# Cached attention on one core: loads in cycles of 16 units, the remainder's P transposed by DMA, and scores up to 14 units ahead

## The chip, the cores and the metric

The kernel runs on one core of one Trainium2 chip. The metric is the device time of one execution in microseconds (us). A core has five engines with a queue of instructions each: PE (matrix multiplication and transposes, with its weight loads shown apart as PEld), DVE (vector operations), ACT (exponential, scaled copies), POOL (elementwise work) and SP, which here only issues loads. They meet through semaphores. Transfers are carried out by 16 DMA engines that are shared by all queues.

## The reference

Two problems of the same shape, A and B, are computed, and their results are put side by side:

```python
B, Sq, D = 16, 144, 448
H, Sk, Dh = 16, 512, 256
q = (x @ wq).reshape(B, Sq, H, Dh).transpose(0, 2, 1, 3)
scores = jnp.einsum("bhqd,bhkd->bhqk", q, k_cache) * (Dh ** -0.5)
p = softmax(scores, axis=-1)
o = jnp.einsum("bhqk,bhkd->bhqd", p, v_cache)
o.transpose(0, 2, 1, 3).reshape(B, Sq, H * Dh) @ wo      # [16, 144, 448]
...
return jnp.concatenate([a, b], axis=-1)                  # [16, 144, 896]
```

All inputs are bf16. Each problem has 64 MB of K and 64 MB of V.

## The kernel before

A **unit** is one head of one batch: 144 queries against 512 keys of 256 elements. There are NT = 512 units, 256 of A and then 256 of B. Four units share one load of V (a group G, 128 of them), eight share one load of K (a supergroup SG, 64 of them).

The 144 queries are more than the 128 rows of PE, so each unit is split: its first 112 queries (QA) have scores of their own, and the remaining 32 (QB) of four units are packed into one set of 128 rows. For one unit PE does, by the names that the program gives its pieces:

- **Q**: the query projection, 8 matmuls (L411), evacuated and scaled by DVE (L425) or ACT (L429).
- **SA**: scores of the 112 queries, 2 matmuls 128x512 (L536) into one of two PSUM banks `sa_ps`. Then the negated maximum on DVE (L548), the exponential with its sum on ACT (L559), the reciprocal on DVE (L569), and the normalization on POOL (L577).
- **TA**: 4 transposes of the normalized P (L590), into the `sa_ps` bank of the unit's parity, and a copy to `pt_sb` by DVE (L600).
- **PV**: P times V, 8 matmuls (L623), evacuated by ACT into `ring` (L638).
- **OP**: the output projection, in pieces of 2 matmuls 128x448 (L661), spread by a credit (`OP_RATE`, 2.25 matmuls a slot), evacuated (L679), and stored.

The packed remainder has, for each supergroup, **SB** (16 matmuls, L459) and, for each group, maximum (L473), exponential (L483), reciprocal (L493), normalization on POOL (L501) and **TB**: 4 transposes of `pb_sb` on PE (L513), then a copy by DVE into `pt_sb` (L522). So there are 128 TBs, 512 transposes.

The order on every engine is written out by one loop over slots (`while True` near the end of the function). In slot i, PE does Q of unit i + LQ = i + 15, SA of unit i + LS = i + 5, TA of unit i + LT = i + 2, and PV of unit i. `_Sched.add` records the reads and writes of each piece, and derives the semaphore waits.

Loads have all one queue, SP, in the order of `dma_plan`. Each has a deadline in slots, an earliest slot `lo` (when its buffer comes free) and a lead; the plan sorts them by deadline. K comes by `dma_start_transpose` (L379) into one of three buffers, V by plain loads (L392) into one of three, x transposed for four batches at a time (L299, L300) into one of three. The weights wq (L277, L279) and wo (L287) of B replace those of A as their parts come free. Stores of finished rows (L691) go out from POOL's queue, and the last two from SP's.

At the start K of 16 units and the first x are loaded as they lie and transposed on PE (KT, L359; XT, L336, in three parts, the last in slot 10), and PE begins with matmuls on zeros (W0, L440) that read `ident` from POOL and `pt_sb`, which DVE clears (L254, `warmz`); DVE also clears a quarter of `wq_sb` (L259, `wqz`).

Of the kernel before, what the change touches and what calls it, by code (L numbers as in the profile page):

```python
# [122 lines left out]
def bass_concat_heads__mha_block_cached__gqa_block_cached__near_ridge_kernel(  # L123
# [18 lines left out]
    NP = 2  # L142
# [7 lines left out]
    NG = NT // 4  # L150
    HG = H // 4
# [9 lines left out]
    LQ, LS, LT = 15, 5, 2  # L161
    LSB = 7
    NKT = 16
    N_WARM = (10, 6)
    NK, NV, NXG = 3, 3, 3
    XB = 4 if Bn % 4 == 0 else (2 if Bn % 2 == 0 else 1)
    NQT, NPA, NPB, NPT, NST, NSTB, NOST = 12, 5, 2, 8, 4, 2, 3
# [5 lines left out]
    NSG = NT // 8  # L173
# [4 lines left out]
    with contextlib.ExitStack() as es:  # L178
# [9 lines left out]
        kt_sb = sb("kt_sb", [128, NK, KR, 2, 8 * SK // KR], BF16)  # L188
        v_sb = sb("v_sb", [128, NV, 4, 4 * DH], BF16)
# [3 lines left out]
        pb_sb = sb("pb_sb", [128, NPB, SK], BF16)  # L193
        pt_sb = sb("pt_sb", [128, NPT, 4, SQ], BF16)
        ost_sb = sb("ost_sb", [128, NOST, D], BF16)
        ident = sb("ident", [128, 128], BF16)
        ones = sb("ones", [128, 128], BF16)
# [8 lines left out]

        S = _Sched()
        kt0_nat = kt_sb[:, 2].rearrange("p k d r -> p (k d r)").rearrange("p (u c e) -> p u c e", u=8, c=4)
        wo_flat = wo_sb[:].rearrange("p c e -> p (c e)")
        kt1_nat = wo_flat[:, 0:8 * 4 * DH].rearrange("p (u c e) -> p u c e", u=8, c=4)  # L210
        x_nat = wo_flat[:, 8 * 4 * DH:8 * 4 * DH + 5 * D].rearrange("p (t e) -> p t e", t=5)
        kt_nat = (kt0_nat, kt1_nat)
        sem_names = list(COMPUTE) + ["ostt0", "ostt1", "xn0", "xn1", "kn0", "kn1", "kn2", "kn3"]
        for i in range(NK):
            sem_names.append("kt%d" % i)
# [8 lines left out]
        for i in range(NOST):  # L224
            sem_names.append("ost%d" % i)
        sems = {n: es.enter_context(nc.semaphore("s_" + n)) for n in sem_names}
# [10 lines left out]

        NEG, RSUM, RINV = 0, NST, 2 * NST
# [3 lines left out]
        def t_ident():  # L242
            def e1(g):
                return g.memset(ones[:], 1.0)
            S.add(POOL, e1, writes=[("ones", 0)], name="ones")

            def e2(g):
                return g.affine_select(ident[:], ones[:], pattern=[[1, 128]], compare_op=ALU.is_equal,
                                       fill=0.0, base=0, channel_multiplier=-1)
            S.add(POOL, e2, reads=[("ones", 0)], writes=[("ident", 0)], name="ident")  # L250

# [30 lines left out]
        def t_load_wo(pr, wg):  # L282
            c0 = wg * WOG
            w = wos[pr]

            def e(q):
                return q.dma_start(wo_sb[:, c0:c0 + WOG, :],  # L287
                                   w[c0 * 128:(c0 + WOG) * 128, :].rearrange("(c p) n -> p c n", p=128)).then_inc(
                    sems["wo%d" % wg], 16)
            x = [(("kn", 2), 1), (("kn", 3), 1), (("xn", 0), 1), (("xn", 1), 1)] if pr == 0 else []  # L290
            S.add(SP, e, writes=[(("wo", wg), pr)] + x, dma_sem="wo%d" % wg, name="wo%d.%d" % (pr, wg))

        def t_load_x(XG):
# [7 lines left out]
            S.add(SP, e, writes=[(("xt", sl), XG)] + ([(("xt2", 0), 1)] if XG == NXG else []), dma_sem="xt%d" % sl, n_dma=2, name="x%d" % XG)  # L301

        def t_load_x_nat(k):
            x = xs[0][0:XB].rearrange("b q d -> (b q) d")
            sem = sems["xn%d" % k]

            def e(q):
                if k == 0:
                    return q.dma_start(x_nat[:, 0:3, :], x[0:384, :].rearrange("(t p) d -> p t d", p=128)).then_inc(
                        sem, 16)  # L310
                q.dma_start(x_nat[:, 3, :], x[384:512, :]).then_inc(sem, 16)
                return q.dma_start(x_nat[0:XB * SQ - 512, 4, :], x[512:XB * SQ, :]).then_inc(sem, 16)
            S.add(SP, e, writes=[(("xn", k), 0)], dma_sem="xn%d" % k, n_dma=1 + k, name="xn%d" % k)
# [10 lines left out]
        def t_xt(k):  # L324
            key, bank, acc = ((("sbb", 0), "sb0", ptb_ps[0]), (("sbb", 1), "sb1", ptb_ps[1]),
                              ("opp", "op", op_ps.bitcast(BF16)))[k]
            c0, n = ((0, 256), (256, 128), (384, XB * SQ - 384))[k]
            dst = acc[:, 0:4 * n].rearrange("p (c r) -> p c r", c=4)

            def e(t):  # L330
                ins = None
                for r0 in range(0, n, 128):
                    m = min(128, n - r0)
                    for kc in range(4):
                        d0 = min(128 * kc, D - 128)
                        ins = t.transpose(dst[:, kc, r0:r0 + m], x_nat[0:m, (c0 + r0) // 128, d0:d0 + 128],  # L336
                                          ident[0:m, 0:m])
                return ins
            S.add(PE, e, reads=[(("xn", k // 2), 0), ("ident", 0)], writes=[(key, ("x", k))], banks=[bank], name="XT%d" % k)

            def ev(v):
                o = xt_sb[:, 0, :, c0:c0 + n]
                return v.activation(o, dst, AF.Copy) if k == 1 else v.tensor_copy(o, dst)
            S.add(ACT if k == 1 else DVE, ev, reads=[(key, ("x", k))], writes=[(("xt2" if k == 2 else "xt", 0), 0)], banks=[bank],
                  name="ext%d" % k)

        def t_kt(u):
# [18 lines left out]
            def ev(v):  # L366
                o = kt_sb[:, u // 8].rearrange("p k d r -> p (k d) r")[:, :, (u % 8) * 128:(u % 8 + 1) * 128]
# [4 lines left out]
        def t_load_k(SG):  # L372
            pr, b, h = unit(8 * SG)
            r0 = b * H + h
            sl = SG % NK
            src = ks[pr].rearrange("b h k d -> (b h k) d")[r0 * SK:(r0 + 8) * SK, :]

            def e(q):
                return q.dma_start_transpose(kt_sb[:, sl].rearrange("p k d r -> p (k d) r"),  # L379
                                             src.rearrange("(r k) d -> r (k d)", k=KR)).then_inc(sems["kt%d" % sl], 16)  # L380
# [5 lines left out]
        def t_load_v(G):  # L386
            pr, b, h0 = unit(4 * G)
            sl = G % NV
            src = vs[pr][b, h0:h0 + 4].rearrange("u (p c) d -> p u (c d)", p=128)

            def e(q):
                return q.dma_start(v_sb[:, sl, :, :], src).then_inc(sems["v%d" % sl], 16)  # L392
            S.add(SP, e, writes=[(("v", sl), G)], dma_sem="v%d" % sl, name="v%d" % G)

# [3 lines left out]
        def t_q(U):  # L398
# [7 lines left out]
            def e(t):  # L406
                ins = None
                for kc in range(4):
# [6 lines left out]
            S.add(PE, e, reads=[(("wq", hg), pr), ("wqz", 0), (("xt", xsl), XG)]  # L415
                  + ([(("xt2", 0), 0)] if XG == 0 and b > 1 else []),
                  writes=[(key, ("q", U))], banks=[bank], name="Q%d" % U)

        def t_evac_q(U):
# [3 lines left out]
            if (U - LQ) % 8 in (2, 4, 6, 7):  # L423
# [7 lines left out]

        def kt_of(U, dc):
            n = SK // KR
            return kt_sb[:, (U // 8) % NK, :, dc, (U % 8) * n:(U % 8 + 1) * n]
# [9 lines left out]

        def kt_keys(us):
            if us[0] < NKT:
                return [(("ktn", u), 0) for u in us]
            return [(("kt", us[0] // 8 % NK), us[0] // 8)]

        def t_sb(SG):  # L450
            ksl = SG % NK

            def e(t):
                ins = None
                for dc in range(2):
                    for jj in range(8):
                        U = 8 * SG + jj
                        j = jj % 4
                        ins = t.matmul(sb_ps[jj // 4][32 * j:32 * j + 32, :].rearrange("q (k r) -> q k r", k=KR),  # L459
                                       lhsT=qt_sb[:, U % NQT, dc, QA:SQ],  # L460
                                       rhs=kt_of(U, dc), start=(dc == 0), stop=(dc == 1),
                                       tile_position=(0, 32 * j))
# [15 lines left out]
        def t_exp_b(G):  # L478
            sl = G % NSTB
            psl = G % NPB  # L480

            def e(a):
                return a.activation(pb_sb[:, psl, :], sb_ps[G % 2][:, :], AF.Exp,  # L483
# [3 lines left out]
                  writes=[(("pb", psl), (G, 0)), (("rsumb", sl), G)], banks=["sb%d" % (G % 2)], name="exb%d" % G)  # L487
# [8 lines left out]
        def t_norm_b(G):  # L496
            sl = G % NSTB
            psl = G % NPB

            def e(g):  # L500
                return g.tensor_tensor(pb_sb[:, psl, :], pb_sb[:, psl, :],  # L501
                                       stat[:, RINVB + sl:RINVB + sl + 1].to_broadcast([128, SK]), op=ALU.mult)
            S.add(POOL, e, reads=[(("pb", psl), (G, 0)), (("rinvb", sl), G)], writes=[(("pb", psl), (G, 1))],
                  name="nmb%d" % G)

        def t_tb(G):
            psl = G % NPB

            def e(t):
                src = pb_sb[:, psl, :].rearrange("q (c p) -> q c p", c=4)  # L510
                ins = None
                for c in range(4):
                    ins = t.transpose(ptb_ps[G % 2][:, c * 128:(c + 1) * 128], src[:, c, :], ident[:, :])  # L513
                return ins
            S.add(PE, e, reads=[(("pb", psl), (G, 1)), ("ident", 0)], writes=[(("sbb", G % 2), ("t", G))],
                  banks=["sb%d" % (G % 2)], name="TB%d" % G)

        def t_evac_ptb(G):
            s0 = (4 * G) % NPT

            def e(v):
                return v.tensor_copy(pt_sb[:, s0:s0 + 4, :, QA:SQ],  # L522
                                     ptb_ps[G % 2][:, 0:512].rearrange("p (c j q) -> p j c q", c=4, j=4))
            S.add(DVE, e, reads=[(("sbb", G % 2), ("t", G))],
                  writes=[(("ptb", (4 * G + j) % NPT), 4 * G + j) for j in range(4)], banks=["sb%d" % (G % 2)],
                  name="eptb%d" % G)

        def t_sa(U):
            SG = U // 8
            ksl = SG % NK  # L530
# [51 lines left out]
        def t_ta(U):  # L582
            psl = U % NPA
            bank = U % 2
# [10 lines left out]
        def t_evac_pta(U):  # L595
            sl = U % NPT
            bank = U % 2
# [15 lines left out]
        def t_pv(U):  # L613
            G, j = divmod(U, 4)
            vsl = G % NV
# [3 lines left out]
            def e(t):  # L619
                ins = None  # L620
                for dc in range(2):
                    for c in range(4):
                        ins = t.matmul(ot_ps[ob][:, dc * SQ:(dc + 1) * SQ],  # L623
                                       lhsT=v_sb[:, vsl, j, c * DH + dc * 128:c * DH + (dc + 1) * 128],
# [60 lines left out]
        def t_store(r):  # L685
            pr, row0, m = chunk_rows(r)
            sl = r % NOST
            sem = "ostt%d" % tail_chunks.index(r) if r in tail_chunks else "ost%d" % sl

            def e(q):  # L690
                return q.dma_start(of[row0:row0 + m, pr * D:(pr + 1) * D], ost_sb[0:m, sl, :]).then_inc(  # L691
                    sems[sem], 16)
            S.add(SP if r in tail_chunks else POOL, e, reads=[(("ost", sl), r)], dma_sem=sem, name="st%d" % r)
# [3 lines left out]
        t_warm_zero()  # L697
        t_wqzero()
        t_ident()
# [252 lines left out]
```

## Time and profile before

| what | us |
|---|---|
| median of 3 runs (1189.49 to 1192.02) | 1189.74 |
| the profiled execution | 1193.1 |
| its span, first to last instruction | 1191.4 |
| ACT busy | 754.9 |
| POOL busy | 676.3 |
| PE, 512 transposes of TB (L513) by their mean of 218 ns | 111.6 |
| POOL, 128 normalizations of the remainder (L501) | 132.9 |
| K, issue to landing, min / median / max | 10.6 / 15.0 / 21.1 |
| V, issue to landing, min / median / max | 5.1 / 6.0 / 15.4 |

The granted clock of TensorE was 1.000 over the whole span. A matmul's duration as listed (218 ns for a TB transpose) covers its way through the array, and matmuls follow each other faster than that: what one costs on PE is read from start to start on the timeline. Waits of SP are mostly those for a buffer to come free. In rows of the timeline a bracket holds the idle time of the engine before the instruction and what ended it; "x4" means four instructions shown as one row.

### The profile page before, as it was taken

To read this page: it belongs to the slowest core of one execution; us is meant where nothing else is said; L and a number is where in the kernel's file an instruction comes from. 1 tells how busy PE (TensorE), PEld (TensorE's weight loads), DVE (VectorE), ACT (ScalarE), POOL (GpSimd) and SP (SyncE) were. 2 spreads that over 40 slices of the span, in tenths; PEclk is the share of its full clock that TensorE was granted. 3 is DMA by queue.
4 is the path that set the end of the run, shared out by engine and by line. 5 is a ranking of instruction groups with operands and counts; after the bars stand their busy time and mean duration, and the time that the engine had idled before them with its cause. 6 is when DMAs were issued, how large, how long until landed. Compare 5 with 4: busy or idle time off the path is not lost.

```text
span 1191.4 us, 34160 instructions
## 1 busy us (share of the span) xinstructions
PE 1178.3 (99%) x14116; PEld 902.6 (76%) x14116; DVE 776.0 (65%) x2192; ACT 754.9 (63%) x2220; POOL 676.3 (57%) x680
## 2 busy tenths in 40 slices
PE   8999999999999999999989999999999999999998
PEld 6777777777777777777767777777777777777775
DVE  5766667666666666666666666666766666666564
ACT  4766666666666666666656666666666666666564
POOL 2555556565565565565555655655655656656553
PEclk9999999999999999999999999999999999999999
DMA  9999999999989999999999999999999999998971
GB/s 343 235 298 279 272 270 234 243 243 253 255 219 246 229 264 249 221 235 244 273 281 286 270 279 277 249 238 233 248 254 234 231 243 250 248 236 238 238 190 48
DMA packets 611146, 294.09 MB, mean 247 GB/s; under 512 B 529712, under 2 KB 538736, under 8 KB 610992
## 3 DMA queue, kind: packets, MB, share of 16 engines
q1 hardware_dynamic: 609360, 288.01, 103.1%
q0 software_dynamic: 1632, 3.90, 1.0%
q8 instruction: 112, 1.84, 0.6%
q14 instruction: 42, 0.34, 0.1%
HBM read 153.61 MB, written 4.13 MB: 132 GB/s over the span
## 4 chain that ended last, share of the span: by engine, by line
PE 95%; DMA 2%; DVE 2%; ACT 0%; issue 0%; SPq 0%; POOL 0%; DVEq 0%; POOLq 0%
PE ot_ps L623 20%; PE qp_ps L411 20%; PE sa_ps L536 19%; PE op_ps L661 17%; PE sa_ps L590 8%; PE sb_ps L459 5%; PE sb_ps L513 2%; DMA kt_sb<-in_A_k_cache_dram 2%; DVE stat L548 1%; DMA wq_sb<-in_B_wq_dram 1%; PE sa_ps L440 0%; PE qp_ps L661 0%; PE op_ps L411 0%; DVE pt_sb L600 0%; DVE stat L473 0%; PE ot_ps L359 0%
## 5 line engine op out<-in xcount | busy, mean ns | idle before, releaser
L577 POOL TENSOR_TENSOR pa_sb<-pa_sb,stat 112x512 bf16<-112x512 bf16 x512 | 531.8, 1039 | 504.1 <-DVE stat L569 503.9
L559 ACT ACTIVATE pa_sb<-sa_ps,stat 112x512 bf16<-112x512 f32 x512 | 351.9, 687 | 404.7 <-DVE stat L548 403.4
L548 DVE TENSOR_REDUCE stat<-sa_ps 112x1 f32<-112x512 f32 x512 | 354.0, 691 | 328.4 <-PE sa_ps L536 327.7
L411 PEld LDWEIGHTS qp_ps<-xt_sb,wq_sb 128*128 128x128 bf16 x4000 | 281.9, 98 | 79.1 <-issue 3.5
L623 PE MATMUL ot_ps<-pt_sb,v_sb 128*128 128x144 bf16 x4096 | 340.5, 226 | 0.0
L411 PE MATMUL qp_ps<-xt_sb,wq_sb 128*128 128x144 bf16 x4000 | 331.8, 226 | 3.1 <-DMA wq_sb<-in_B_wq_dram 3.1
L536 PE MATMUL sa_ps<-kt_sb,qt_sb 128*112 128x512 bf16 x1024 | 310.1, 384 | 1.7 <-ACT pa_sb L559 0.7
L661 PE MATMUL op_ps<-wo_sb,ring 128*128 128x448 bf16 x1120 | 280.6, 352 | 0.0
L623 PEld LDWEIGHTS ot_ps<-pt_sb,v_sb 128*128 128x128 bf16 x4096 | 268.5, 97 | 0.4
L590 PEld LDWEIGHTS sa_ps<-ident,pa_sb 112*128 112x128 bf16 x2048 | 146.7, 97 | 108.2 <-ACT pa_sb L559 21.1
L638 ACT ACTIVATE ring<-ot_ps 128x288 bf16<-128x288 f32 (+8 forms) x512 | 189.9, 371 | 4.5 <-PE ot_ps L623 4.5
L600 DVE COPY pt_sb<-sa_ps 128x448 bf16<-128x448 bf16 x512 | 190.8, 373 | 2.4 <-PE sa_ps L590 2.4
L590 PE MATMUL sa_ps<-ident,pa_sb 112*128 112x112 bf16 x2048 | 185.4, 212 | 0.1
L425 DVE TENSOR_SCALAR qt_sb<-qp_ps 128x288 bf16<-128x288 f32 x247 | 112.8, 457 | 65.9 <-PE qp_ps L411 65.1
L501 POOL TENSOR_TENSOR pb_sb<-pb_sb,stat 128x512 bf16<-128x512 bf16 x128 | 132.9, 1038 | 0.7 <-DVE stat L493 0.7
L536 PEld LDWEIGHTS sa_ps<-kt_sb,qt_sb 128*112 128x112 bf16 x1024 | 97.2, 129 | 37.8 <-issue 27.2
L429 ACT ACTIVATE qt_sb<-qp_ps 128x288 bf16<-128x288 f32 x253 | 104.5, 413 | 15.9 <-PE qp_ps L411 14.8
L661 PEld LDWEIGHTS op_ps<-wo_sb,ring 128*128 128x128 bf16 x1120 | 94.7, 98 | 25.6 <-ACT ring L638 0.2
L559 ACT ACTIVATION_READ_ACCUMULATOR pa_sb<-sa_ps,stat 112x1 f32 x512 | 99.0, 193 | 0.0
L483 ACT ACTIVATE pb_sb<-sb_ps,stat 128x512 bf16<-128x512 f32 x128 | 88.4, 690 | 0.0
L473 DVE TENSOR_REDUCE stat<-sb_ps 128x1 f32<-128x512 f32 x128 | 87.2, 681 | 0.0
L569 DVE RECIPROCAL stat<-stat 112x1 f32<-112x1 f32 x512 | 78.4, 153 | 0.5 <-ACT pa_sb L559 0.5
(49 smaller groups left out, 426.3 us busy)
## 6 DMA issues: line engine op xcount, KB each, us to landing
v_sb<-in_A_v_cache_dram SPq DMA_DIRECT2D x64, 1024.0 KB, 6.0
v_sb<-in_B_v_cache_dram SPq DMA_DIRECT2D x64, 1024.0 KB, 6.0
out_dram<-ost_sb POOLq DMA_DIRECT2D x34, 112.0 KB, 6.1
wo_sb<-in_A_wo_dram SPq DMA_DIRECT2D x8, 448.0 KB, 8.1
wo_sb<-in_B_wo_dram SPq DMA_DIRECT2D x8, 448.0 KB, 6.9
wq_sb<-in_A_wq_dram SPq DMA_DIRECT2D x4, 768.0 KB, 11.0
wq_sb<-in_B_wq_dram SPq DMA_DIRECT2D x4, 768.0 KB, 7.6
kt_sb<-in_A_k_cache_dram SPq DMA_DIRECT2D x2, 1024.0 KB, 8.8
```

What stands on the lines that cost most here:

```text
L411: ins = t.matmul(acc[:, dc * SQ:(dc + 1) * SQ], lhsT=wq_sb[:, kc, c0:c0 + 128], rhs=xt_sb[:, xsl, kc, xo:xo + SQ], start=(kc == 0 and dc = ...
L425: return v.tensor_scalar(qt_sb[:, sl, :, :], src, 1.0 / 16.0, None, op0=ALU.mult)
L501: return g.tensor_tensor(pb_sb[:, psl, :], pb_sb[:, psl, :], stat[:, RINVB + sl:RINVB + sl + 1].to_broadcast([128, SK]), op=ALU.mult)
L536: ins = t.matmul(sa_ps[bank][0:QA, :].rearrange("q (k r) -> q k r", k=KR), lhsT=qt_sb[:, U % NQT, dc, 0:QA], rhs=kt_of(U, dc), start=(dc = ...
L548: return v.tensor_reduce(stat[0:QA, NEG + sl:NEG + sl + 1], sa_ps[bank][0:QA, :], axis=AX.X, op=ALU.max, negate=True)
L559: return a.activation(pa_sb[0:QA, psl, :], sa_ps[bank][0:QA, :], AF.Exp, bias=stat[0:QA, NEG + sl:NEG + sl + 1], scale=1.0, accum_out=stat ...
L577: return g.tensor_tensor(pa_sb[0:QA, psl, :], pa_sb[0:QA, psl, :], stat[0:QA, RINV + sl:RINV + sl + 1].to_broadcast([QA, SK]), op=ALU.mult)
L590: ins = t.transpose(pta_ps[bank][:, c * 128:c * 128 + QA], src[:, c, :], ident[0:QA, 0:QA])
L600: return v.tensor_copy(pt_sb[:, sl, :, 0:QA], pta_ps[bank][:, 0:512].rearrange("p (c q) -> p c q", c=4)[:, :, 0:QA])
L623: ins = t.matmul(ot_ps[ob][:, dc * SQ:(dc + 1) * SQ], lhsT=v_sb[:, vsl, j, c * DH + dc * 128:c * DH + (dc + 1) * 128], rhs=pt_sb[:, sl, c, ...
L638: ins = a.activation(ring[:, 2 * h:2 * h + 2, c0:c0 + n1], src[:, :, 0:n1], AF.Copy)
L661: ins = t.matmul(acc[0:m, 0:D], lhsT=ring[:, c, col0:col0 + m], rhs=wo_sb[:, c, :], start=(c == first), stop=(c == last))
```

## The change

- **P of the remainder by DMA.** TB stays on PE only in supergroups 0 to 9 and 28 to 37 (`TB_SG`). In the other 44, `t_ptb_dma` transposes both groups' `pb_sb` (128 rows of 1024) from SBUF to SBUF into one buffer `pbt_sb`, issued on SP. From supergroup 6 on (`NDIR`), `t_copy_ptb` on POOL copies each group from `pbt_sb` to `pt_sb`; where TB stays after that, DVE's copy goes to `pbt_sb` too.
- **Lead of the scores.** SA runs ahead of PV by `LAGS`: 5 up to supergroup 5, then one more for each supergroup up to 14. For this the 8 SAs of each of nine supergroups lie in 7 slots, so that one slot of each holds two. `NPA` grows from 5 to 14. Q of unit u is in the slot of SA of unit u - 8, or in slot u - 15 if that is earlier. TA's bank is that opposite to the last SA (`ta_bank`).
- **Loads.** From supergroup 10 on (slot 76) a written-out cycle of 16 units: P(n), K(n+2), P(n+1), K(n+3), four V, and x every 32 units. K has three buffers up to supergroup 8 and then two, V three and then five, in one tensor `kv_sb`. x comes two batches at a time in two buffers. Stores are issued on SP, in three slots of each 16.
- **Weights of B.** wo is loaded at slots 277 and 293, and B's output projection starts no earlier than slot 290. `OP_RATE` becomes 2.5.
- **Start.** The third part of XT is gone (the first x has 288 rows), `ones` lies in `pa_sb`, and `t_warm_zero` is called behind `t_wqzero` and `t_ident`.

Counted in the orders of the two programs, PE has 88 TBs and one XT fewer, DVE 2103 pieces in place of 2192, POOL 758 in place of 676, and SP 314 in place of 229.

```diff
-    LQ, LS, LT = 15, 5, 2
-    LSB = 7
+    LT = 2
+    LS = 5
+    LAGS = (5, 5, 5, 5, 5, 5, 6, 7, 8, 9, 10, 11, 12, 13, 14)
+    RAMP = 10
+    NDIR = 6
+    TB_SG = set(range(RAMP)) | set(range(NSG // 2 - 4, NSG // 2 + 6))
+    NK, NV, NXG = 2, 5, 2
+    K3 = 8
+    WO_AT = (277, 277, 293, 293)
+    OP_FROM = (0, 34)
-    NK, NV, NXG = 3, 3, 3
-    XB = 4 if Bn % 4 == 0 else (2 if Bn % 2 == 0 else 1)
-    NQT, NPA, NPB, NPT, NST, NSTB, NOST = 12, 5, 2, 8, 4, 2, 3
+    XB = 2
+    NQT, NPA, NPB, NPT, NST, NSTB, NOST = 12, 14, 2, 8, 4, 2, 3
+    NPBT = 1
...
+        def k_slot(SG):
+            return SG % 3 if SG <= K3 else (SG - K3 - 1) % 2
+
+        def v_slot(G):
+            return G % 3 if G < 2 * K3 + 2 else (G - 2 * K3 + 1) % 5
...
+        def t_ptb_dma(SG):
+            psl = SG % NPB
+            tsl = SG % NPBT
+
+            def e(q):
+                return q.dma_start_transpose(pbt_sb[:, tsl, :, :, :].rearrange("p g c q -> p (g c) q"),
+                                             pb_sb[:, psl, :, :].rearrange("p g k -> p (g k)")).then_inc(
+                    sems["pb%d" % tsl], 16)
...
-        def t_evac_ptb(G):
+        def t_evac_tb(G):
+            tsl = (G // 2) % NPBT
             s0 = (4 * G) % NPT
...
+            if G < 2 * NDIR:
...
+            else:
+                def e(v):
+                    return v.tensor_copy(pbt_sb[:, tsl, G % 2, :, :],
+                                         ptb_ps[G % 2][:, 0:512].rearrange("p (c q) -> p c q", c=4))
...
+        def t_copy_ptb(G):
+            tsl = (G // 2) % NPBT
+            s0 = (4 * G) % NPT
+
+            def e(g):
+                return g.tensor_copy(pt_sb[:, s0:s0 + 4, :, QA:SQ],
+                                     pbt_sb[:, tsl, G % 2, :, :].rearrange("p c (j q) -> p j c q", j=4))
...
-            bank = U % 2
+            bank = ta_bank[U]
...
-            S.add(SP if r in tail_chunks else POOL, e, reads=[(("ost", sl), r)], dma_sem=sem, name="st%d" % r)
+            S.add(SP, e, reads=[(("ost", sl), r)], dma_sem="ost%d" % sl, name="st%d" % r)
...
-        t_warm_zero()
         t_wqzero()
         t_ident()
+        t_warm_zero()
+        ta_bank = {}
+        lag = [LAGS[min(n, len(LAGS) - 1)] for n in range(NSG)]
+        grp_slot = [8 * n - lag[n] for n in range(NSG)] + [8 * NSG - lag[-1] + 4]
+        sb_slot = list(grp_slot)
+        sb_slot[1] = 4
+        sa_slot = [grp_slot[u // 8] + (u % 8) * (grp_slot[u // 8 + 1] - grp_slot[u // 8]) // 8 for u in range(NT)]
...
+        q_slot = [min(sa_slot[max(u - 8, 0)], u - 15) for u in range(NT)]
...
+        for wg in range(NWG):
+            plan(WO_AT[wg // 2], s_min, NU + OP_FROM[1] + wg, t_load_wo, 1, wg)
+        for n in range(RAMP, NSG, 2):
+            t = 8 * n
+            XG = (t + 32) // (XB * H)
+            if (t + 32) % (XB * H) == 0 and XG < NXGT:
+                plan_x(t - (20 if XG == Bn // XB + 2 else 4), XG)
+            plan_pb(t - 4, n)
+            if n + 2 < NSG:
+                plan_k(t - 3, n + 2)
+            plan_pb(t + 2, n + 1)
+            if n + 2 < NSG:
+                plan_k(t + 2, n + 3)
+            for j, at in enumerate((5, 5, 5, 8)):
+                if 2 * n + 3 + j < NG:
+                    plan_v(t + at, 2 * n + 3 + j)
+        for hg in range(HG):
+            lo = q_slot[NU - H + 4 * hg + 3] + 1
+            plan((4.9, 4.9, 8, 16)[hg] + NU - 32, lo, q_slot[NU + 4 * hg], t_load_wq, 1, hg)
...
-        OP_RATE = float(NCH * NWO) / NU
+        OP_RATE = 10.0 / 9 * NCH * NWO / NU
...
-            while stores and stores[0][1] <= i:
+            while stores and stores[0][1] <= i and (i % 16 in (9, 10, 11) or i >= NT - 4):
                 t_store(stores.pop(0)[0])
...
+            if i % 8 == 7 and NDIR * 8 <= i + 1 < NT:
+                t_copy_ptb((i + 1) // 4)
+            if i % 8 == 1 and NDIR * 8 <= i < NT:
+                t_copy_ptb((i + 3) // 4)
...
             if 0 <= u < NT:
+                ta_bank[u] = 1 - last_sa % 2 if sas else u % 2
                 t_ta(u)
...
-                            queue_chunk(r, i + OP_DELAY)
+                            queue_chunk(r, max(i + OP_DELAY, pr * NU + OP_FROM[pr]))
...
-            if i == 10:
-                t_xt(2)
```

## The prediction

> **What bounds the kernel now.** I read the busy line first, then the chain of waits, then what PE waited for.
>
> ```profile
> span 1191.4 us, 34160 instructions
> PE 1178.3 (99%) x14116; PEld 902.6 (76%) x14116; DVE 776.0 (65%) x2192; ACT 754.9 (63%) x2220; POOL 676.3 (57%) x680
> ...
> PE 95%; DMA 2%; DVE 2%; ACT 0%; issue 0%; SPq 0%; POOL 0%; DVEq 0%; POOLq 0%
> ```
>
> PE is busy 99% of the span and carries 95% of the chain: an instruction taken from PE is a gain, a wait given to PE is a loss, and nothing else counts. The waits of PE, the longest first:
>
> ```profile
> PE qp_ps L411 <- DMA wq_sb<-in_B_wq_dram: 3.1, 1, 3.1
> PE sb_ps L459 <- DMA kt_sb<-in_A_k_cache_dram: 1.7, 1, 1.7
> PE sa_ps L440 <- POOL ident L248: 1.5, 1, 1.5
> ```
>
> So only two loads are late in the whole run. The second limit is close, though. The DMA view cut to 254 to 290 us, 0.9 us a slice:
>
> ```profile
> DMA  5499979949699999899999999099999999908999
> GB/s 8 104 290 290 204 230 341 400 178 48 173 407 405 307 290 214 117 221 286 289 288 290 290 291 154 7 330 366 385 380 400 373 361 291 274 6 197 290 290 291
> ```
>
> K's transposes run at 290 GB/s, V's loads at 360 to 400, and between the kinds stand slices of 48, 7 and 6 GB/s. The packets show these as stalls of all 16 engines of about 1.45 us, when a plain load gives way to a transpose or an instruction fetch falls into one: 89 over the run, 118 us, thus 3.7 us per 16 units.
>
> **What is removed.** A unit's slot on the timeline, with a TB and without:
>
> ```profile
> 713.28 0.36 PE L590 MATMUL sa_ps<-ident,pa_sb 112*128 112x112 bf16 x4
> 713.47 0.39 PE L513 MATMUL sb_ps<-ident,pb_sb 128*128 128x128 bf16 x4
> 713.70 0.66 PE L623 MATMUL ot_ps<-pt_sb,v_sb 128*128 128x144 bf16 x8
> ...
> 715.51 0.36 PE L590 MATMUL sa_ps<-ident,pa_sb 112*128 112x112 bf16 x4
> 715.71 0.67 PE L623 MATMUL ot_ps<-pt_sb,v_sb 128*128 128x144 bf16 x8
> ```
>
> The TB holds PE from 713.47 to 713.70, 0.23 us. 44 of 64 supergroups lose two each: 88 x 0.23 = -20.2. XT2's 8 transposes go, at TA's 0.05 each: -0.4. The waits of 3.1 (wq of B) and 1.7 (K of unit 40) are counted out, and what comes in their place is counted below: -4.8. DVE's 88 evacuations (0.41 each) go at no gain by themselves, DVE being 65% busy. Together -25.4.
>
> **What is added on PE's path.**
>
> *Start.* W0 needs `warmz`, which moves behind `wqz` on DVE:
>
> ```profile
> 0.97 0.30 DVE L254 MEMSET pt_sb<- 128x288 uint32 x1
> ...
> 1.52 4.42 PE L440 MATMUL sa_ps<-pt_sb,ident 128*128 128x512 bf16 x10 [1.52 <-POOL ident L248]
> 1.64 1.76 DVE L259 MEMSET wq_sb<- 64x2048 uint32 x1 [0.37 <-issue]
> ```
>
> Now 0.97 + 1.76 + up to 0.37 + 0.30 gives 3.0 to 3.4 in place of 1.52. PE waits for no load at the start (no such row above), so all of it counts: +1.7 (0 to 1.9).
>
> *Ramp of the lead.* From 5 to 14, one per group: 9 slots hold two SAs, and the TA of that slot goes into the bank of the first. How long a bank is taken:
>
> ```profile
> 700.92 0.59 PE L536 MATMUL sa_ps<-kt_sb,qt_sb 128*112 128x512 bf16 x2
> 701.55 0.69 DVE L548 TENSOR_REDUCE stat<-sa_ps 112x1 f32<-112x512 f32 x1 [0.47 <-PE sa_ps L536]
> 702.28 0.69 ACT L559 ACTIVATE pa_sb<-sa_ps,stat 112x512 bf16<-112x512 f32 x1 [0.48 <-DVE stat L548]
> 702.87 0.19 ACT L559 ACTIVATION_READ_ACCUMULATOR pa_sb<-sa_ps,stat 112x1 f32 x1
> ```
>
> Free at 703.06, 2.14 after SA's start. PE meanwhile has SA, Q, SA = 0.43 + 0.50 + 0.43 = 1.36 (starts on the timeline), so it waits 0.8; in the first two groups no Q stands between, 0.86, so 1.3. 7 x 0.8 + 2 x 1.3 = +8.2 (0 if the bank were another one; at most 9 x 1.3 = 11.7).
>
> *Slots without an OP piece.* In PE's two orders, between units 8 and 488, 73 slots have none before, 109 after (OP_RATE 2.5 in place of 2.25, B's pieces held back to unit 290). Such a slot has Q 0.50, SA 0.43, TA 0.20, PV 0.50 = 1.63 us on PE. DVE needs 0.63 to the max, 0.69 for it, 0.37 for the TA's copy, 0.15 for a reciprocal: 1.84. So 0.2 x 36 = 7.2. From the other side: the gaps over 0.1 us before SA sum to 6.6 us over the 73 slots, 0.09 each, so 3.3. I take +7, nearer the chain, because DVE's queue has no slack where such slots follow each other; ends 0 and 14.
>
> *Tail.* The last 14 slots, not 5, have no Q and SA: TA 0.20 and PV 0.50 against copies of 0.37 and 0.40 with hand-overs of some 0.2. Nine more slots at 0 to 0.45: I take +2.
>
> **DMA.** New are 44 transposes of P (256 KB) on SP, 116 POOL copies, and 2 K buffers for 3. No row shows an SBUF-to-SBUF transpose. Lower end: 1024 packets at K's rate (8192 in 7.3 us) 0.9 us. Upper end: a stall of 1.45 on either side, 3.8. In the packets of 268.27 us, K follows x's transpose without a gap, so I take 0.9. A cycle of 16 units then needs 2 x 7.3 (K) + 2 x 0.9 (P) + 4 x 2.7 (V) + 3.7 (stalls) + 0.9 (x, store) = 31.8 us, against 16 x 2.268 (mean slot, units 112 to 216) - 4 x 0.23 = 35.4. It fits, with 3.6 us to spare, but with two buffers K(n+2) must land within 9 slots of its release, about 20 us, and it waits on SP behind P(n), which itself waits for the POOL copy; behind them queue P(n+1), K(n+3) and four V. K's present landing:
>
> ```profile
> L379 SPq DMA_TRANSPOSE kt_sb<-in_B_k_cache_dram x32: 7880/12758/17200, 573.8 to 1136.4; - x32
> ...
> DMA to landing us min/median/max: 10.6/15.0/21.1
> ```
>
> Ordinary cycles hold: 15.0 + 0.9 of 20. Three places don't. At unit 40, K5 was 1.7 late and now has one piece of x and its stall more in its way: 3. At SG 32, wq of B (three loads of 0.9 MB before K32, 2.4 each at V's rate) makes 39 us of a 36 us cycle: 3.5. At SG 38, four loads of wo (1.2 each) make 36.6 of 35.4, after a queue already late: 2.5. Sum +9; ends 0 (queue ahead everywhere) and 25 (each 8 late, K's landing spread and a stall). PV of 80 waits for the first copy, as the first P follows four V: +1.5 (0 to 3).
>
> The POOL copies (about 1 us by its norm's 1038 ns) cost nothing: POOL is 57% busy and 14 units of lead cover it; without that cover each late copy would hold the norms behind it, then TA.
>
> The Trainium skill, page "DMA: Bandwidth & Descriptors", section "Anatomy of one DMA — SWDGE (gpsimd) path", puts about 2.0 us of fixed cost on each DMA beside its bytes, and the section "Latency and other measured facts" gives a DMA transpose 261 GB/s. By both, an estimate for P is 3.0 us, and the sum would end with the third case below. The trace disagrees on the rate (290 here), and the gapless packets at 268.27 us speak against a fixed part that holds the engines.
>
> **Sum.** -25.4 + 1.7 + 8.2 + 7 + 2 + 9 + 1.5 = +4.0: span 1195.4. The profiled execution was 1.7 over its span and the median 1.7 below the span, so the median comes to 1193.7; I say 1194.
>
> **Rivals.**
> 1. *No load is late.* Grouping by kind halves the changes from plain to transpose; K32 lands in time if two of its stalls fall away. Then the 9 falls and the OP-free slots cost their measured 3.3: 1194 - 9 - 3.7 = 1181 to 1185, say 1184 (1176 to 1187). For: slack of 3.6 us a cycle. Against: K5 was already late. It decides once K of SG 32 and 38 land before their SB.
> 2. *DMA becomes the bound.* From P = 0.9 + 3.6/2 = 2.7 us a cycle is longer than its 16 slots, and every cycle ends in a wait of SB for K. At 3.0 us, 0.6 x 22 cycles = 13: 1207; at 3.5 us, 1.6 x 22: 1229. I say 1209 (1203 to 1229). For: 103% of the DMA time is already taken on the main queue. Against: the gapless packets. This is also the case of the skill's fixed cost.
> 3. *It does not do what it says*: P lands so late that the copies, the norms and TA follow each other; the gain of 20.2 is paid back in TA's waits: about 1192.
>
> **How the numbers follow.** Forecast 0.48, own range 1188 to 1201 (slower 0.35, same 0.11, faster 0.02). No load late 0.28 (faster 0.26, same 0.02). DMA bound 0.19, all slower. The last 0.05 (same 0.02, slower 0.03). Under 0.2%, 2.4 us, a measurement of this kernel tells no difference. The range reaches from inside the first rival, 1181, to 1213.
>
> **What would show it.** PE's instructions 352 fewer and its busy time about 20.6 lower; first matmul at 3.2; nine TA waits on ACT of about 0.8 between units 40 and 110; SB waits for K at units 40, 256 and 304 and nowhere else; P's packets spanning about 0.9 us. Wrong if SB waits for K every 16 units (rival 2), or never (rival 1), or if TA waits on POOL (rival 3).

## The result: 1.2% slower, and the profile after

| | before | after |
|---|---|---|
| median, us | 1189.74 (1188.88 to 1192.02, 5 runs) | 1204.10 (1200.88 to 1205.55, 5 runs) |
| profiled execution / its span, us | 1193.1 / 1191.4 | 1204.98 / 1203.3 |
| PE busy, us | 1178.3 | 1170.9 |
| K, issue to landing, min / median / max, us | 10.6 / 15.0 / 21.1 | 9.7 / 12.1 / 21.3 |

The ratio after to before is 1.0115, with an interval of 1.0096 to 1.0134. The same lines of the page as before, then what PE waited for (us in total, times, longest):

```profile
span 1203.3 us, 33501 instructions
PE 1170.9 (97%) x13756; PEld 881.1 (73%) x13756; DVE 751.3 (62%) x2103; ACT 753.8 (63%) x2220; POOL 721.2 (60%) x762
...
PE 83%; DMA 8%; DVE 4%; POOL 3%; ACT 1%; issue 1%; SPq 0%; DVEq 0%
```

```profile
PE sa_ps L628 <- ACT pa_sb L597: 7.8, 10, 1.2
PE sb_ps L474 <- DMA kv_sb<-in_B_k_cache_dram: 6.9, 3, 3.5
PE sb_ps L474 <- DMA kv_sb<-in_A_k_cache_dram: 4.1, 3, 2.4
PE sa_ps L453 <- DVE pt_sb L276: 3.5, 1, 3.5
```

PE has 360 instructions fewer (352 of TB, 8 of XT), yet its part of the chain fell from 95% to 83%: DMA, POOL, DVE and ACT now end what PE waits for. The first two kinds of wait are new or have grown. PE's busy time fell by only 7.4 us, although 19.8 us of TBs are gone: some 12 us of the gaps found below lie under the listed durations of matmuls and count as busy.

To find all of it, I took from both traces, for each piece of PE, the time from its start to the next piece's start, less the pace that the same pair keeps when nothing holds it (SA 0.43, Q 0.50, TA 0.20, PV 0.50, an OP piece 0.38, SB 0.98). These excesses sum to 23.1 us before and 54.3 after:

| excess of PE, us | before | after |
|---|---|---|
| between the two SAs of a double slot and TA | 0 | 8.5 |
| ahead of SB (K) | 1.9 | 11.9 |
| ahead of Q of unit 268 (wq of B) | 3.3 | 0 |
| ahead of PV of unit 80 (first POOL copy) | 0 | 0.8 |
| slow clock behind two K waits | 0 | 3.3 |
| small waits of 0.05 to 0.3 elsewhere, most ahead of SA or Q where no OP piece stands | 3.7 | 10.7 |
| after unit 480 | 2.2 | 4.6 |
| below 0.05 each, the first 24 units and others | 12.0 | 14.5 |

So 31.2 us of new gaps stand against 19.8 us of removed TBs (88 x 0.225) and nearly equal small changes at the start. The spans differ by 11.9.

The largest new wait, in the timeline of a double slot, where the two SAs are those of units 56 and 57:

```profile
144.67 0.64 PE L574 MATMUL sa_ps<-kv_sb,qt_sb 128*112 128x512 bf16 x2
145.14 0.66 PE L429 MATMUL qp_ps<-xt_sb,wq_sb 128*128 128x144 bf16 x8
145.64 0.59 PE L574 MATMUL sa_ps<-kv_sb,qt_sb 128*112 128x512 bf16 x2
146.90 0.37 PE L628 MATMUL sa_ps<-ident,pa_sb 112*128 112x112 bf16 x4 [0.67 <-ACT pa_sb L597]
```

TA could start at 145.64 + 0.43 = 146.07 and starts at 146.90. The trace puts the end of its wait down to ACT's exponential of the first SA, whose sum is read out until 146.85.

And what nobody had counted, in windows of 2 us around SB of units 256 and 304 (columns: length, busy time and instructions of PE, PEld, DVE, ACT, POOL; then the granted clock, DMA share and GB/s):

```profile
592.00:594.00 2.00, 0.21 (x4) 0.15 (x8) 0.00 (x0) 0.00 (x0) 0.00 (x0) 1.00 1.10 273
594.00:596.00 2.00, 2.00 (x18) 0.72 (x11) 0.00 (x0) 0.00 (x0) 0.00 (x0) 0.52 1.01 315
596.00:598.00 2.00, 2.00 (x17) 1.54 (x16) 1.47 (x4) 0.74 (x3) 0.63 (x1) 0.63 0.99 125
598.00:600.00 2.00, 2.00 (x26) 1.61 (x25) 1.17 (x3) 1.01 (x4) 0.41 (x1) 1.00 1.38 106
...
706.00:708.00 2.00, 1.77 (x17) 0.67 (x18) 0.00 (x0) 0.00 (x0) 0.00 (x0) 0.68 1.27 290
708.00:710.00 2.00, 2.00 (x15) 1.62 (x14) 1.23 (x4) 0.50 (x1) 0.39 (x1) 0.50 1.27 290
```

PE stands for want of K and, when it goes on, runs at about half the clock for some 3 us: 15 to 18 matmuls in 2 us in place of 26.

### The profile page after: what moved, and what is told of

Its sections match the earlier page's. It is cut to its first block, busy times and chain, and to the rows that moved or that the text cites. A ratio compares the mean times of both kernels' runs of the same rounds, so it can differ in the third digit from the quotient of the medians.

```text
span 1203.3 us, 33501 instructions
## 1 busy us (share of the span) xinstructions
PE 1170.9 (97%) x13756; PEld 881.1 (73%) x13756; DVE 751.3 (62%) x2103; ACT 753.8 (63%) x2220; POOL 721.2 (60%) x762
## 4 chain that ended last, share of the span: by engine, by line
PE 83%; DMA 8%; DVE 4%; POOL 3%; ACT 1%; issue 1%; SPq 0%; DVEq 0%
PE ot_ps L661 18%; PE qp_ps L429 17%; PE sa_ps L574 17%; PE op_ps L699 16%; PE sa_ps L628 7%; PE sb_ps L474 5%; DMA kv_sb<-in_B_k_cache_dram 4%; DMA kv_sb<-in_A_k_cache_dram 4%; DVE stat L586 2%; POOL pa_sb L615 2%; ACT pa_sb L597 1%; POOL pb_sb L515 1%; PE sb_ps L537 1%; PE qp_ps L699 1%; DVE pt_sb L638 0%
## 5 line engine op out<-in xcount | busy, mean ns | idle before, releaser
L661 PE MATMUL ot_ps<-pt_sb,kv_sb 128*128 128x144 bf16 x4096 | 341.5, 226 | 0.7 <-POOL pt_sb L563 0.7
L574 PE MATMUL sa_ps<-kv_sb,qt_sb 128*112 128x512 bf16 x1024 | 312.2, 387 | 3.4 <-DVE pt_sb L638 1.6
L699 PE MATMUL op_ps<-wo_sb,ring 128*128 128x448 bf16 x1120 | 274.9, 353 | 0.0
L661 PEld LDWEIGHTS ot_ps<-pt_sb,kv_sb 128*128 128x128 bf16 x4096 | 268.9, 98 | 1.2 <-POOL pt_sb L563 0.8
L628 PEld LDWEIGHTS sa_ps<-ident,pa_sb 112*128 112x128 bf16 x2048 | 143.8, 97 | 121.4 <-ACT pa_sb L597 40.3
L574 PEld LDWEIGHTS sa_ps<-kv_sb,qt_sb 128*112 128x112 bf16 x1024 | 96.5, 129 | 44.5 <-issue 27.6
L474 PE MATMUL sb_ps<-kv_sb,qt_sb 128*32 128x512 bf16 x1024 | 68.1, 386 | 12.2 <-DMA kv_sb<-in_B_k_cache_dram 6.9
## 6 DMA issues: line engine op xcount, KB each, us to landing
wq_sb<-in_A_wq_dram SPq DMA_DIRECT2D x4, 768.0 KB, 11.9
```

The lines of the kernel that those rows point to most:

```text
L574: ins = t.matmul(sa_ps[bank][0:QA, :].rearrange("q (k r) -> q k r", k=KR), lhsT=qt_sb[:, U % NQT, dc, 0:QA], rhs=kt_of(U, dc), start=(dc = ...
L628: ins = t.transpose(pta_ps[bank][:, c * 128:c * 128 + QA], src[:, c, :], ident[0:QA, 0:QA])
L661: ins = t.matmul(ot_ps[ob][:, dc * SQ:(dc + 1) * SQ], lhsT=v_sb[vsl][:, j, c * DH + dc * 128:c * DH + (dc + 1) * 128], rhs=pt_sb[:, sl, c, ...
L699: ins = t.matmul(acc[0:m, 0:D], lhsT=ring[:, c, col0:col0 + m], rhs=wo_sb[:, c, :], start=(c == first), stop=(c == last))
```

## The experiments

Times are medians; the ratio to the runs of before on the same chip has its interval behind it. The changed kernel's is 1.0115.

### TB back on PE in all supergroups

```diff
-    TB_SG = set(range(RAMP)) | set(range(NSG // 2 - 4, NSG // 2 + 6))
+    TB_SG = set(range(NSG))
```

> The changed kernel, but TB stays on PE in all 64 supergroups and no P is transposed by DMA. Theory (the removed TBs give what was counted, P's transposes cost next to nothing): 88 x 0.225 = 19.8 us come back, the waits of SB for K at units 176 and 336 (1.1 and 0.8) may go, so the time rises by 18 to 20 us, to about 1222. Rival (P's transposes load the DMA queue so that K is late all over): most of the K waits of 11.7 us go with them, the time rises by 8 to 12, to about 1214.

1219.30 us, 1.0243 (1.0221 to 1.0265): 0.0128 more than the changed kernel, 15.2 us. That lies between the two ranges, a little nearer the theory's. The gaps ahead of SB fell from 11.9 to 9.4 and the slow clock remained behind one wait only, so 19.8 of TB came back less some 4.5 of gaps. P's transposes by DMA are thus not free, but they are worth 15 us on PE.

### TA of double slots in another bank

```diff
+        def ta_acc(U):
+            bank = ta_bank[U]
+            if bank == 2:
+                return ptb_ps[0], ("sbb", 0), "sb0"
+            return pta_ps[bank], ("sap", bank), "sa%d" % bank
...
-                ta_bank[u] = 1 - last_sa % 2 if sas else u % 2
+                ta_bank[u] = 2 if len(sas) == 2 and 8 < i < 112 else 1 - last_sa % 2 if sas else u % 2
```

In `sa_slot`, the second SA of a slot moves from the first to the last slot of its supergroup.

> The changed kernel with the second SA of the nine double slots at the end of its supergroup, and the TA of that slot written into a free bank of SB's. Theory (the bank is what PE waits for in double slots): the nine waits of 0.83 to 1.33 us before TA, 8.5 us together, go and nothing takes their place: about 1195.5. Rival (DVE and ACT can't follow two SAs in a slot whatever the bank, so the wait moves to the next SA or SB): within 2 us of the changed kernel, 1202 to 1206.

1198.11 us, 1.0058 (1.0035 to 1.0081): 6.8 us less by the ratios, of the 8.5 expected. The waits before TA are gone but for one in the tail, which the changed kernel has too:

```profile
PE sb_ps L474 <- DMA kv_sb<-in_B_k_cache_dram: 5.7, 4, 2.4
PE sb_ps L474 <- DMA kv_sb<-in_A_k_cache_dram: 5.1, 6, 2.2
...
PE sa_ps L634 <- ACT pa_sb L597: 0.8, 1, 0.8
```

So the wait hung on the bank of the double slot's first SA. The edit also moves the second SA, and no run separates the two. Ten waits for K now stand where there were six (K of unit 112 is 2.2 late), but they sum to 10.8 us against 11.0. What is missing from the 8.5 is rather in small waits: in six of the double slots PE now stands 0.28 us ahead of Q, so a little of what the rival said is true.

### Other orders of loads

```diff
-    WO_AT = (277, 277, 293, 293)
+    WO_AT = (277, 285.1, 293, 293)
...
-        first += [("wo", w) for w in range(4)] + [("v", 6), ("k", 4), ("v", 7)]
-        first += [("wo", w) for w in range(4, 8)] + [("v", 8), ("k", 5), ("v", 9), ("v", 10), ("x", 2)]
+        first += [("wo", w) for w in range(3)] + [("v", 6), ("k", 4), ("v", 7), ("wo", 3), ("wo", 4), ("k", 5), ("v", 8)]
+        first += [("wo", w) for w in range(5, 8)] + [("v", 9), ("v", 10), ("x", 2)]
...
-                    plan_v(t + at, 2 * n + 3 + j)
+                    plan_v(t + (13.05 if j == 3 and n in (28, 34) else at), 2 * n + 3 + j)
```

> The changed kernel with the same loads in another order at three places: K of units 32 and 40 ahead of three to five of A's wo loads, K of unit 256 ahead of one V, K of unit 304 ahead of one V and two of B's wo loads. Theory (these K waits, 0.7 + 2.5 + 2.8 + 3.5 us, come from the plain loads queued ahead, and the slow clock behind the two longest, some 3.3 us, from the waits): 9 to 12 us less, about 1193. Rival (the DMA engines have no time to spare there, so what is put behind K is late in K's place): less than 3 us gained, 1201 or more.

1202.98 us, 1.0108 (1.0086 to 1.0130): no difference that the intervals tell. By the time the rival is right, by what is late in the trace both are:

```profile
PE op_ps L699 <- DMA wo_sb<-in_A_wo_dram: 5.7, 1, 5.7
...
PE sb_ps L474 <- DMA kv_sb<-in_B_k_cache_dram: 2.8, 2, 1.8
PE sb_ps L474 <- DMA kv_sb<-in_A_k_cache_dram: 1.7, 2, 1.2
```

None of the four waits for K that were aimed at is left (gaps ahead of SB 5.4 in place of 11.9), so they did come from the plain loads ahead. At the start, though, wo is 5.7 late in K's place, with a slow clock behind it. K of unit 208 is 1.2 late, and at the change to B K of units 272 and 320 are 1.8 and 1.1 late: between PV of units 240 and 320 this order still saved 5.8 us.

### Matmuls that fill the wait

```diff
+            if SG in (32, 38):
+                def d(t):
+                    ins = None
+                    for _ in range(28):
+                        ins = t.matmul(sb_ps[0][:, 0:128], lhsT=ident[:, :], rhs=ident[:, :], start=True, stop=True)
+                    return ins
+                S.add(PE, d, reads=[("ident", 0)], writes=[(("sbb", 0), ("d", SG))], banks=["sb0"], name="D%d" % SG)
```

> The changed kernel with 28 matmuls of 128x128 on the identity (about 1.6 us, results overwritten) ahead of the SBs of units 256 and 304, where PE waits 2.8 and 3.5 us for K. Theory (the granted clock of 0.5 for some 3 us behind these waits comes from PE being idle for so long): K is as late as before, but the clock stays at 1.00 and 3.3 us are gained, about 1201. Rival (the clock falls for another reason, or PE's idle time is not what counts): clock dips and time as in the changed kernel, 1204.

1202.13 us (1200.66 to 1206.95), 1.0108 (1.0073 to 1.0142): its time can't be told from the changed kernel's. The trace can:

```profile
588.00:590.00 2.00, 1.27 (x23) 1.10 (x20) 0.00 (x0) 0.16 (x1) 0.00 (x0) 1.00 1.14 285
590.00:592.00 2.00, 0.63 (x12) 0.39 (x16) 0.00 (x0) 0.00 (x0) 0.00 (x0) 1.00 0.99 312
592.00:594.00 2.00, 2.00 (x25) 1.27 (x18) 0.97 (x4) 0.25 (x1) 0.13 (x1) 1.00 1.23 112
```

PE is idle for 2.10 us ahead of SB of unit 256, where it was idle for 2.70 in the changed kernel's execution, and the clock behind it stays at 1.00; its mean is 1.000 in three of four runs, against 0.996 to 0.999 in all five of the changed kernel. At unit 304 K came almost in time in this execution (0.4), so that place tells nothing. That fits the theory, but it rests on one place and on the mean clock of four runs, and the gain in time is not shown. The last section has what the clocks of all traces say of it.

### The lead left at 5, with TB on PE

```diff
-    LAGS = (5, 5, 5, 5, 5, 5, 6, 7, 8, 9, 10, 11, 12, 13, 14)
-    NDIR = 6
+    LAGS = (5,)
+    NDIR = 64
```

Beside the edit of the first experiment; x and wq of B are issued at their earliest slot where the plan's slot came too soon for the shorter lead, and K(n+2) and K(n+3) go out eight slots apart.

> The changed kernel with TB on PE in all supergroups (1219.3 so far) and besides that the lead of the scores left at 5, so that no slot holds two SAs, no POOL copy is needed, and the last group's SAs are spread as the others. What is left of the change is the order of loads with two K buffers, the stores on SP, the output projection's rate and the start. Theory (the lead costs its nine bank waits of 8.5, the thin tail of 2.4, and the late first copy of 0.8): 1219.3 - 11.7 = about 1207.5. Rival (a lead of 5 leaves K too little time between the release of one of two buffers and its use): the bank waits go, but waits of SB for K take their place, 1215 or more.

1197.53 us, 1.0066 (1.0047 to 1.0086): 0.0177 less than with the lead (the first experiment's 1.0243), 21 us and not 11.7.

```profile
PE sb_ps L474 <- DMA kv_sb<-in_B_k_cache_dram: 3.0, 2, 1.8
```

By excess, the bank waits (8.5), gaps ahead of SB (9.4 to 3.3), the slow clock (1.3), the tail (2.6) and small waits (4.2) went. The rival falls: two K buffers and a lead of 5 are no trouble. How much of the 6 us at SB is the lead's, and how much that of the K loads that no longer go out in pairs, this run does not separate. It gives the change's balance, though: everything beside the lead and P's way costs 0.0066, 7.9 us; the lead, with the POOL copies and the pairs of K loads that come with it, adds 21, and transposing P by DMA takes back 15. The small waits are worth a second look. Slots without an OP piece are the same in number here as in the changed kernel, and all small waits between units 8 and 488 stand in such slots: 5.3 us in 74 slots before (0.07 each), 8.1 in 110 here (0.07 each), 12.4 in 110 in the changed kernel (0.11 each). So the lead made each of them dearer.

### P's transposes left out

```diff
-            if SG not in TB_SG:
+            if False:
                 plan(at, sb_slot[SG] + 5, 8 * SG - 1, t_ptb_dma, SG)
```

> The changed kernel without P's 44 transposes by DMA: they are left out and nothing takes their place, so the POOL copies pass on an older remainder (the last 32 queries of these units come out other than in the reference). Theory (P costs the DMA queue about 1 to 2.4 us each, out of a slack of 3.6 us per 16 units, and what PE pays are the K waits at units 176 and 336 and part of the others): 2 to 5 us less than the changed kernel, 1199 to 1202. Rival (the DMA queue is the bound and P's transposes are what makes it so): the K waits and the slow clock behind them go, 11 to 15 us less, 1189 to 1193.

1197.75 us, 1.0069 (1.0049 to 1.0089): 5.5 us less by the ratios, by the width of the intervals not to be told from the theory's 2 to 5, and far from the rival's 11. The trace has 4.5 us less of gaps, 2.8 of them ahead of SB; 8.3 us of waits for K stay. P's DMA in the changed kernel:

```profile
L525 SPq DMA_TRANSPOSE pbt_sb<-pb_sb x44: 1231/1649/4381, 210.5 to 1170.6; - x44
...
DMA to landing us min/median/max: 3.0/5.2/10.1
```

From its first packet to its last a P takes 1.0 us at best (behind x's transpose), about 1.5 ahead of K(n+3), and 2.0 to 3.3 where it follows V or a store. On PE that comes to 5.5 / 44 = 0.13 us each, against 0.45 for the two TBs that it replaces.

### Together

`e_mix1` has the bank, `warmz` first, x behind K(n+2), and loads in an order of their own at the start and at B:

```diff
-            plan_x(t - (20 if XG == Bn // XB + 2 else 4), XG)
+            plan_x(t - (20 if XG == Bn // XB + 2 else 2.9), XG)
...
-    OP_FROM = (0, 34)
+    OP_FROM = (33, 34)
...
+        first += [("k", 4), ("v", 6), ("wo", 0), ("v", 7), ("wo", 1), ("k", 5), ("wo", 2), ("v", 8)]
+        first += [("wo", w) for w in range(3, 8)] + [("v", 9), ("v", 10), ("x", 2)]
```

> The changed kernel with the TA of double slots in SB's bank (1198.1 alone), warmz first on DVE, x issued behind K(n+2) and not ahead of it, K of units 32 and 40 ahead of most of A's wo loads with A's output projection from slot 33 on, and one V and two wo loads behind K of units 256 and 304. Theory (each of these waits has its own cause in what is queued ahead): from 1198.1 go 1.0 (start), 0.7 (K of unit 40), 4.3 (K in the x cycles, units 112, 176, 336, 464) and 7.5 (K of units 256 and 304 with the slow clock behind them): about 1184.6. Rival (the DMA engines are the bound, so a wait that is taken away at one K comes back at the next): 1194 or more, with SB's waits for K at other units.

1191.36 us, 1.0015 (1.0003 to 1.0026). Both are partly right: SB's gaps are down to 1.8, but V of unit 32 is 4.7 late in K's place.

`e_mix2` spreads the output projection as well (`WO_AT` and `OP_FROM` of B move by a few slots too):

```diff
-        OP_RATE = 10.0 / 9 * NCH * NWO / NU
+        OP_RATE = 1.0 * NCH * NWO / NU
...
-            if i >= u_tail0 - 14:
+            if i >= u_tail0 - 1:
```

> The run before this one, with the output projection's rate back at 2.25, no extra pieces in the 14 slots ahead of the tail, and B's projection from slot 293: 61 slots without a piece between units 8 and 488 in place of 106, and one in place of twelve after unit 480. Theory (slots without a piece cost about 0.1 each, the tail's 2.4 come from them too): 4 to 6 us less than the run before, 1179 to 1181. Rival (the pieces take as much time wherever they stand, and the small waits before SA are hidden elsewhere): within 1.5 us of it.

1186.25 us (1182.29 to 1188.45), 0.9960 (0.9947 to 0.9973): 5.1 less than `e_mix1`, as the theory had it, though both stand higher than forecast. In the traces small waits fell from 13.2 to 7.1 and those after unit 480 from 4.6 to 2.0, while gaps ahead of SB rose from 1.8 to 6.0. The execution traced here took 1183.0 us, 3.3 less than the median, so these sums are not those of the medians. What is left:

```profile
PE ot_ps L667 <- DMA kv_sb<-in_A_v_cache_dram: 4.9, 2, 4.1
PE sb_ps L474 <- DMA kv_sb<-in_B_k_cache_dram: 4.2, 3, 1.7
```

Two more orders of the first loads were tried on top of it. `e_mix3` puts V ahead of K and all of A's wo behind both (A's projection from slot 36); `e_mix4` goes back to the changed kernel's first loads and to its projection of A.

> e_mix2 with V of unit 32 ahead of K of unit 40 and all of A's wo loads behind both (A's projection from slot 36), B's wo loads two at a time behind K of units 304 and 312, and TB on PE in supergroups 38 and 39 too. Theory (the wait of 4.3 us before PV of unit 32 and of 1.0 before PV of unit 24 came from the V loads standing behind K of unit 40; the wait of 1.7 at unit 320 from P and wo ahead): 5 to 7 us less than e_mix2, less 0.9 for four TBs put back: about 1181. Rival (in the first 100 us the DMA engines are the bound, so that some load is late in any order): K of unit 40 or wo is late in V's place, 1184 or more.

1190.91 us (1183.54 to 1195.33), 0.9996 (0.9978 to 1.0014). The rival holds: K of unit 48 is now 5.7 late, more than V was, and V of unit 36 is 1.7 late.

```profile
PE sb_ps L474 <- DMA kv_sb<-in_B_k_cache_dram: 6.8, 5, 2.7
PE sb_ps L474 <- DMA kv_sb<-in_A_k_cache_dram: 6.7, 2, 5.7
```

> e_mix2 with A's first loads and A's output projection as in the changed kernel again (wo ahead of K of units 32 and 40, projection from the first finished rows on). Theory (the first 100 us have no free DMA time, so some load is late in any order, and K late by 0.7 and 2.5 is cheaper than V late by 1.0 and 4.3 with a slow clock behind it): 3 to 4 us less than e_mix2's 1186.3, about 1183. Rival (what is saved there comes back as waits for K behind it): 1185 or more.

1186.20 us (1182.88 to 1191.05), 0.9962 (0.9942 to 0.9981): the same as `e_mix2`. In the traced execution B's K is waited for longer (7.4 us, the longest 3.9, in place of 4.2), as the rival had it. So in the first 125 us some load is late in every order that was tried, and 0.4% under before is as far as these edits go.

## Why the prediction was right, and where it was short

The direction held, and so did the terms by kind: the gain of the TBs is there and more than eaten by the lead's bank waits, slots without an OP piece, the tail and late K loads. The size did not hold. A rise of 4 us was forecast and 14.4 were measured. The time lies in the range over all cases, 1181 to 1213, but 3 us above the forecast's own, 1188 to 1201, and just inside that of the second rival, whose sign (SB waiting for K every 16 units) is absent. A sum of -25.4 and +29.4 was small against the uncertainty of its terms, so that its sign came out right is in part luck.

| step | predicted, us | in the trace |
|---|---|---|
| 88 TBs | -20.2 | -19.8 |
| XT2 and start | +1.3 | +0.5 |
| waits of wq and K of unit 40 counted out | -4.8 | -5.2 |
| nine double slots | +8.2 | +8.5 |
| slots without an OP piece | +7 | +7.0 |
| tail | +2 | +2.4 |
| K late | +9 | +11.9 |
| first copy | +1.5 | +0.8 |
| slow clock behind waits | not counted | +3.3 |
| gaps below 0.05 and single others | not counted | +2.5 |
| sum | +4.0 | +11.9 |

**What was right.** The bank wait was worked out as 2.14 - 1.36 = 0.8 and 1.3, and is 0.83 seven times and 1.33 twice; the experiment with another bank took it away.

**What agrees by luck.** The term of the slots without an OP piece came out at its 7.0, but not for its reason. 36 more such slots at 0.2 us each were to make it. With the lead at 5 the same slots stand without a piece and their small waits are only 2.8 us above before, near the prediction's other price (3.3); the rest hangs on the lead, by a way that no run shows. That the waits stand in these slots, the traces do show, and from `e_mix1` to `e_mix2` they fell with the number of such slots.

**The start** is 1.0 late at the first PV, not 1.7, and not all of the delay counted. The first matmul comes 1.94 later, but the ten matmuls on zeros and XT's twelve transposes take 0.9 less: full clock is on record from 6.57 us before and from 6.97 after, and W0's matmuls take 0.42 us each ahead of that and 0.22 behind it. So only 3.5 us of PE's work pass at the slow pace in place of 5.0, and XT, now on 96 rows and not 128, falls wholly behind it (0.52 us, before 1.07).

**The late K loads** were named at units 40, 256 and 304 with 3, 3.5 and 2.5; they are 2.5, 2.8 and 3.5, together 8.8. "Nowhere else" was wrong: units 32, 176, 296 and 336 add 0.7, 1.1, 0.2 and 0.8. The reason given for unit 40, a piece of x ahead, was wrong as well: x stands behind that K on SP. What stood ahead were wo and V, as `e_order` showed.

**What was missing.** A wait was priced at its own length. Behind two of them the clock fell to half for 3.4 us, which cost 1.6 us each. The sign "busy time about 20.6 lower" failed too (7.4), as the listed durations hide part of the new gaps. The page of the Trainium skill "TensorE: Matmul & The Clock Gate", section "HAM oscillation — how this bites in real kernels", warns of idle gaps over about 3.4 us. Here the rows decide: the clock fell after 2.70 us, and in `e_tb` after 2.21.

**The level.** The median was set 1.7 below the predicted span, as in before. But the profiled execution of before lay 3.4 above its median, that of after only 0.9. That makes 2.5 us of the miss of 10.4 (1193.7 to 1204.1), and the sum 7.9.

**The rivals.** "DMA becomes the bound" was half of what happened. A P took 1.8 us of packets on the mean, twice the 0.9 of the sum but short of the turning point of 2.7, and the ordinary cycles hold: SB waits in two of 22, at most 1.1 us. But the slack was small enough that P's 44 transposes cost 5.5 us on PE, and that from `e_mix1` to `e_mix2` part of the gain on PE came back as waits for K.

The fixed 2.0 us that the Trainium skill gives (page "DMA: Bandwidth & Descriptors", section "Anatomy of one DMA — SWDGE (gpsimd) path") did not hold the engines: in all but a few cycles K's first packet comes right behind P's last. That section is on DMAs issued from gpsimd, while P goes out on SP, and it puts most of the 2.0 us down to completion, not to the engines, so the prediction read more into it than it says.

"No load is late" failed at the named places. Its reason, that grouping by kind halves the changes, does not show in the stalls either: counted as packets over 1.0 us, sixteen of them to a stall, they are 89 before and 88 after. "It does not do what it says" fell, with one wait for a POOL copy of 0.7 us.

## What to carry to other kernels

- Where one engine is busy 99% of the time, taking 20 us of work from it is only worth what the next resource can feed. Work out that resource's slack at its worst places (start, change of weights), not in an ordinary cycle.
- A deeper lead has a price: here nine slots with twice the scores cost 8.5 us through two PSUM banks, and a free third bank for that one slot took most of it away. But the lead and what came with it cost 21 us in all, more than the 15 that transposing P by DMA gave back.
- A wait of PE may cost more than its length; look at the granted clock behind it.
- A term of a sum that comes out right may be right by luck. Look for a run in which its stated reason is there and the rest is not, as the slots without an OP piece in the run with the lead at 5.

## What the runs showed of the hardware

The granted clock changes on a grid. In each trace all its changes lie multiples of 3.413 us apart, and where the grid starts differs from one execution to the next. What counts is PE's idle time inside one stretch of the grid. Here are two neighbouring stretches of after at unit 256, then two of before at the wait for wq of B (columns as in the result):

```profile
590.65:594.06 3.41, 0.71 (x16) 0.46 (x17) 0.00 (x0) 0.41 (x1) 0.00 (x0) 1.00 1.18 283
594.06:597.48 3.42, 3.42 (x29) 1.87 (x22) 0.95 (x3) 0.22 (x1) 0.11 (x1) 0.50 1.00 245
...
597.07:600.49 3.42, 1.53 (x17) 0.90 (x14) 1.61 (x6) 2.46 (x7) 2.40 (x3) 1.00 1.04 330
600.49:603.90 3.41, 2.19 (x30) 1.93 (x30) 1.07 (x4) 0.75 (x2) 0.23 (x1) 1.00 1.29 170
```

After's 2.70 us of idle time lie in one stretch, and the next runs at half the clock. Before's 3.10 us are cut into 1.88 and 1.22 by the edge, and the clock stays. Over all twelve traces, some 4100 stretches at full clock, there is no exception: the clock fell behind each of the 13 that had 2.01 us of idle time or more, and behind none with 1.88 or less. What lies between was not met. The fall lasted one stretch, or a second one in the four cases in which PE was idle for 0.78 us or more in the first. So the length of a wait alone does not decide: 2.21 us at unit 256 in `e_tb` fell into one stretch and brought the clock down, 2.18 us at unit 304 were cut in half and did not.

This bears on the matmuls that fill the wait. Without them PE would have been idle for 2.8 us of one stretch (an estimate: from the end of Q at 587.70 to the edge at 590.53); with them it was idle for 1.25 there. By this pattern the fillers did keep the clock up, at that one place.

A DMA transpose from SBUF to SBUF of 128 x 1024 bf16 took 1.0 us of packets (256 KB) right behind another transpose. K's landing is shorter in the changed kernel (median 15.0 to 12.1 us), where transposes are issued one behind the other, with V's loads together behind them; that this order is the reason was not tested.
